# An order for TensorE written by hand through three quarters of a fused attention and FFN kernel, and router gates moved behind the scaling of v

## The chip, the cores and the metric

The kernel runs on one core of a Trainium2 chip. The metric is the device time of one execution in microseconds (us); less is better. TensorE is called PE here, its weight loads PEld, VectorE DVE, ScalarE ACT, GpSimd POOL, and SyncE SP (it issues most DMAs).

## What is computed

Three stages follow each other, for 4 batches of 576 tokens:

```
scores = q @ k^T / 8 + (cum[i] - cum[j])       # 8 heads of 64, causal, cum = cumsum(log f)
x      = softmax(scores) @ v                   # first attention, heads side by side: 512 wide
u      = x + (x^T @ U @ V)^T                   # mixing along the tokens, rank 32
y      = u + relu(u @ w_ch1) @ w_ch2           # FFN, 512 -> 2048 -> 512
logits = y @ w_gate                            # 4 experts, the best 2 chosen per token
out    = sum over chosen e of gate_e * softmax(causal(y wq_e (y wk_e)^T / 8)) @ (y wv_e) @ wo_e
```

## The kernel before

Everything is kept transposed and split into a high and a low part where full precision is wanted, so that most products are made of three matrix products (high x high, high x low, low x high).

**First attention.** The 32 heads go in 16 pairs, numbered 0 to 15 here; four pairs make a batch. For a pair `load_pair`, `split_high` and `split_low` bring q and k into one of two sets of head tiles (`qa, qb, ka, kb`), `value_scale` and `value_parts` scale v and split it (`vh`, `vl`). `row_max` (two PSUM tiles `ua`, `ub`; the maxima on DVE; a turn `mt` on PE; a row `mr` that two DMAs copy into row 66 of `qa`) makes the softmax's maxima ahead of the scores. `scores` makes two PSUM tiles `sc` per head; ACT takes the exponentials (`pf`), ACT makes the high half (`ph`) and DVE the low half (`pl`). `weighted_values` is 45 products into `av`, then DVE normalises into `x`. After both heads `mix` adds the rank-32 product (`gp`, `g`, `up`) and ACT's queue sends the pair's rows of u to DRAM (`udram`).

**FFN.** `ffn_stream` is a generator. Each of its steps is one group of 12 products of 128x288, either `hps` (`ffn_hidden`, line 367) or `cps` (`ffn_out`, line 382); 256 groups make the whole FFN. The weights come in four quarters; `load_quarter_steps` narrows each piece of them on DVE and ACT (tile `wst`) and makes the low half on POOL (`w1l`, `w2l`). `fill(n)` takes n groups; it is called during the first attention from pair 4 on, since batch 0 is through the attention by then. The rest of the FFN runs behind the attention.

**Second attention.** Four experts per batch: `project` (`pq`), `expert_values` (`pv`, then `gates`, `value_scale`, `value_parts`), and the same `row_max`, `scores` and `weighted_values`.

**What sets the order.** In the first attention and the FFN a scheduler orders all engines at build time, by a model of the instructions; the program only says what depends on what. For pair p the program asks for the other head of the pair before and `mix` of it, the maxima of pair p+1 and the scores of pair p in turn, the values of p+1, the inputs of p+2, the first head's weighted values, some steps of the weights (`WRATE`), and then eight FFN groups in one go (none at pair 4, three at pair 15). The second attention is under `tc.manual_schedule` for PE: PE's order there is the program's, with one or two groups of other work (`work_on`) between the steps of a head. On each engine the instructions run in the order they were given, and an instruction that waits holds all that are behind it on its engine.

The PSUM tiles `ua`, `ub`, `sc` share two buffers (`ps2`), `av` has one, and `hps, cps, gp, up, mt, amt, rsp` share three (`psf`).

Of the kernel before, what the change touches and what calls it, by code (L numbers as in the profile page):

```python
# [8 lines left out]
F32 = mybir.dt.float32  # L9
# [8 lines left out]
P = 128  # L18
# [18 lines left out]
VEXP = 8192.0  # L37

WRATE = (0, 0, 1, 4, 4, 4, 3)
FIRST = 0  # L40
LAST = 3
BIG = -1.0e30
NEG = -3.0e38
ISC = 0.125
# [13 lines left out]
def kernel(  # L58
# [417 lines left out]
    def pair_heads(p):  # L476
        return heads[2 * (p % 2)], heads[2 * (p % 2) + 1]
# [43 lines left out]
    def values(p):  # L521
        if p >= NPAIR:
            return
        vr = st_in[p][1]
        st_rs[p] = drain(value_scale(vr[:]))
        value_parts(vr[:], st_rs[p], *vhs[p % 2])

    def maxima(p, j):
        if p < NPAIR:
            cur["last"] = drain(row_max(pair_heads(p)[j], next_mx()))  # L530

    def attend(p, j):
        vh, vl = vhs[p % 2]
# [5 lines left out]
    def mix(p):  # L539

        b, m, x = p // NP, p % NP, xs[p]
        gp = psf.tile([3 * R, P], F32, name="gp", tag="f")
        for t in range(NT):
            k = 64 if t == NT - 1 else P
            nc.tensor.matmul(gp[:], ut[0:k, t, :], x[0:k, t, :], start=t == 0,  # L545
                             stop=t == NT - 1)
        g = sx.tile([3 * R, P], F32R, name="g")
        nc.scalar.copy(g[:], gp[:])
        nc.vector.tensor_tensor(g[R:2 * R, :], gp[R:2 * R, :], f32(g[R:2 * R, :]), OP.subtract)
        ust = sx.tile([P, S], F32, name="ustage")  # L550
        for (t0, t1, c0, c1) in ((0, 2, 0, 256), (2, 5, 256, S)):
            up = psf.tile([P, 512], F32, name="up", tag="f")
            nc.tensor.matmul(up[:, 0:c1 - c0], g[:], vs[:, c0:c1], start=True, stop=False)
            for t in range(t0, t1):
                k = 64 if t == NT - 1 else P
                nc.tensor.matmul(up[:, t * P - c0:t * P - c0 + k], x[0:k, t, :],
                                 ident[0:k, 0:k], is_transpose=True, start=False,
                                 stop=t == t1 - 1)
            nc.scalar.copy(ust[:, c0:c1], up[:, 0:c1 - c0])
        nc.scalar.dma_start(udram[b, :, m, :], ust[:])  # L560
# [1 line left out]
    load_pair(0)  # L562
    split_high(0)
    split_low(0)
    values(0)
    maxima(0, 0)
    maxima(0, 1)
    load_pair(1)
    split_high(1)
    split_low(1)  # L570
# [49 lines left out]
    load_weights(wy_pool, 1)  # L620
    with tc.issue_after(cur["last"].ins):
        load_mix()
    for p in range(NPAIR + 1):
        if p < NPAIR:
            xs[p] = sx.tile([P, NT, P], F32, name="x", bufs=2)
        if p > 0:
            attend(p - 1, 1)
            mix(p - 1)
        if p == NP:
            sin0.release()  # L630
            att0.release()
            pre.release()
            cur["att"] = att
            fu = cur["fu"] = pool("fu", 2, "right")
            fh = cur["fh"] = pool("fh", 8, "right")
            fy = cur["fy"] = pool("fy", 3, "right")
        if p > 0 and p % NP == 0:
            ffn_prepare(p - NP)
            if p == NP:
                ffn_prepare(1)  # L640
        if p == NPAIR:
            break
        maxima(p + 1, 0)
        st_p[p, 0] = drain(scores(pair_heads(p)[0]))
        maxima(p + 1, 1)
        st_p[p, 1] = drain(scores(pair_heads(p)[1]))
        values(p + 1)
        load_pair(p + 2)
        split_high(p + 2)
        split_low(p + 2)  # L650
        attend(p, 0)
        if p < len(WRATE):
            with tc.issue_after(cur["last"].ins):
                more_weights(WRATE[p])
        if p >= NP:
            fill({NP: FIRST, NPAIR - 1: LAST}.get(p, 8))
    hpool.release()
    att.release()
    sin.release()
# [131 lines left out]
    def expert_values(b, y):  # L791

        yh, yl = y
        vr = sy.tile([P, NT, NV], F32, name="vr3", bufs=1)
        v0 = 2 * E * D
        for t in range(NT):
            pv = psf.tile([P, 512], F32, name="pv", tag="f")
            ts_ = slice(t * P, t * P + P)
            n = 0
            for k in range(KT):  # L800
                for ya, wa in ((yh, wah), (yh, wal), (yl, wah)):
                    nc.tensor.matmul(pv[:, 0:NV], ya[:, k, ts_], wa[:, k, v0:v0 + NV],  # L802
                                     start=n == 0, stop=n == 3 * KT - 1)
# [12 lines left out]

    def turn_outputs(b, m, oh, ol):
# [69 lines left out]
    def head_max(h):  # L887
        b, e = divmod(h, E)
        return row_max(pair_of(b, e // 2)[e % 2], next_mx())

    def one(gen):
        next(gen, None)

# [120 lines left out]
```

## Time and profile before

| what | before |
|---|---|
| median of 3 runs | 988.1 us (987.05 to 991.45) |
| the profiled execution, its own time | 991.99 us |
| its span from first to last instruction | 990.1 us |
| PE busy | 885.4 us (89%) |
| DVE / ACT / POOL busy | 558.2 / 414.6 / 286.7 us |
| mean granted PE clock | 0.906 |
| pair 4's first scores | starts at 104.4 us |
| first FFN group | starts at 151.49 us |
| last `mix` ends, the FFN alone follows | 462.5 us |

Busy time counts an instruction from its start to its end. [...] A wait "a <- b" is idle time in front of a that ended when b did.

### The profile page before, as it was taken

To read this page: it belongs to the slowest core of one execution; us is meant where nothing else is said; L and a number is where in the kernel's file an instruction comes from. 1 tells how busy PE (TensorE), PEld (TensorE's weight loads), DVE (VectorE), ACT (ScalarE), POOL (GpSimd) and SP (SyncE) were. 2 spreads that over 40 slices of the span, in tenths; PEclk is the share of its full clock that TensorE was granted. 3 is DMA by queue.
4 is the path that set the end of the run, shared out by engine and by line. 5 is a ranking of instruction groups with operands and counts; after the bars stand their busy time and mean duration, and the time that the engine had idled before them with its cause. 6 is when DMAs were issued, how large, how long until landed. Compare 5 with 4: busy or idle time off the path is not lost.

```text
span 990.1 us, 19003 instructions
## 1 busy us (share of the span) xinstructions
PE 885.4 (89%) x7480; PEld 825.4 (83%) x7480; DVE 558.2 (56%) x1468; ACT 414.6 (42%) x784; POOL 286.7 (29%) x238
## 2 busy tenths in 40 slices
PE   4888878789899998999999999999999686999997
PEld 3777768778888987998998899999998686888875
DVE  7777577877355556453245653222225667666654
ACT  4565555555244444242224342222103543545543
POOL 8444354333332224110324342423022303000010
PEclk9786569889888999899999999999999797989968
DMA  6434445443423242202258663424006220212111
GB/s 182 116 82 123 134 135 165 132 125 105 143 71 85 78 132 66 56 13 74 72 186 300 213 220 112 144 70 126 25 25 180 61 49 7 73 31 74 37 43 55
DMA packets 68777, 101.94 MB, mean 103 GB/s; under 512 B 6608, under 2 KB 49424, under 8 KB 68688
## 3 DMA queue, kind: packets, MB, share of 16 engines
q1 hardware_dynamic: 64416, 92.47, 31.8%
q10 hardware_dynamic: 4272, 8.26, 2.3%
q8 instruction: 59, 0.97, 0.4%
q14 instruction: 30, 0.25, 0.1%
HBM read 60.33 MB, written 22.56 MB: 84 GB/s over the span
## 4 chain that ended last, share of the span: by engine, by line
PE 72%; DVE 13%; DMA 5%; ACT 4%; issue 3%; POOL 2%; SPq 0%; ACTq 0%; POOLq 0%; DVEq 0%
PE hps L367 19%; PE cps L382 19%; PE sc L210 9%; DVE pl L221 3%; PE av L237 3%; PE pq L759 3%; PE pv L802 3%; PE po L838 3%; PE av L241 2%; PE av L239 2%; PE gp L545 2%; DMA ust<-udram 2%; DVE junk L174 2%; PE ub L163 2%; ACT pf L219 1%
## 5 line engine op out<-in xcount | busy, mean ns | idle before, releaser
L382 PE MATMUL cps<-hh,w2h 128*128 128x288 f32 x512 | 153.2, 300 | 4.6 <-DVE yc L384 3.5
L382 PE MATMUL cps<-hh,w2l 128*128 128x288 f32 x512 | 151.6, 296 | 0.0
L382 PE MATMUL cps<-hl,w2h 128*128 128x288 f32 x512 | 150.6, 294 | 0.0
L367 PE MATMUL hps<-uh,w1h 128*128 128x288 f32 x512 | 144.9, 304 | 0.0
L367 PE MATMUL hps<-uh,w1l 128*128 128x288 f32 x512 | 143.5, 301 | 0.0
L221 DVE TENSOR_TENSOR pl<-pf,ph 128x576 f16<-128x576 f32 x144 | 121.4, 850 | 34.7 <-ACT ph L220 34.5
L372 DVE SCALAR_TENSOR_TENSOR hl<-hps,hh 128x288 fp32r<-128x288 f32 x128 | 58.2, 455 | 145.6 <-ACT hh L371 145.5
L371 ACT ACTIVATE hh<-hps 128x288 fp32r<-128x288 f32 x128 | 52.3, 408 | 195.9 <-PE hps L367 190.1
L219 ACT ACTIVATE pf<-sc 128x576 f32<-128x576 f32 x144 | 84.5, 612 | 85.0 <-PE sc L210 64.9
L210 PE MATMUL sc<-qa,ka 67*128 67x288 f32 (+4 forms) x288 | 88.4, 367 | 24.6 <-ACT pf L219 13.1
L237 PE MATMUL av<-vh,ph 128*128 128x65 f16 x720 | 103.6, 211 | 7.1 <-DVE x L283 5.1
L241 PE MATMUL av<-vh,pl 128*128 128x65 f16 x720 | 100.8, 208 | 2.4 <-DVE pl L221 1.7
L239 PE MATMUL av<-vl,ph 128*128 128x64 f16 x720 | 101.5, 207 | 0.0
L382 PEld LDWEIGHTS cps<-hh,w2h 128*128 128x128 f32 x512 | 96.4, 189 | 5.7 <-DVE yc L384 4.1
L367 PEld LDWEIGHTS hps<-uh,w1h 128*128 128x128 f32 x512 | 98.8, 193 | 1.2 <-issue 0.9
L367 PEld LDWEIGHTS hps<-uh,w1l 128*128 128x128 f32 x512 | 99.2, 194 | 0.0
L382 PEld LDWEIGHTS cps<-hh,w2l 128*128 128x128 f32 x512 | 96.3, 188 | 0.0
L382 PEld LDWEIGHTS cps<-hl,w2h 128*128 128x128 f32 x512 | 96.3, 188 | 0.0
L237 PEld LDWEIGHTS <-ph 128*128 128x128 f16 x720 | 74.5, 107 | 19.3 <-DVE x L283 4.7
L220 ACT CAST ph<-pf 128x576 f16<-128x576 f32 x144 | 88.9, 639 | 1.7
L367 PE MATMUL hps<-ul,w1h 128*128 128x288 f32 x512 | 89.2, 297 | 0.0
L210 PEld LDWEIGHTS sc<-qa,ka 67*128 67x128 f32 x288 | 60.3, 231 | 30.0 <-ACT pf L219 15.1
(160 smaller groups left out, 2018.1 us busy)
## 6 DMA issues: line engine op xcount, KB each, us to landing
raw<-in_w_dram SPq DMA_DIRECT2D x32, 512.0 KB
ust<-udram SPq DMA_DIRECT2D x22, 576.0 KB
qkt<-in_qk_dram SPq DMA_DIRECT2D x16, 576.0 KB
yc<-ydram SPq DMA_DIRECT2D x14, 576.0 KB
ydram<-yc SPq DMA_DIRECT2D x14, 576.0 KB
vr<-in_v_dram SPq DMA_DIRECT2D x16, 320.0 KB
udram<-ustage ACTq DMA_DIRECT2D x16, 288.0 KB
ydram<-ust SPq DMA_DIRECT2D x8, 576.0 KB
```

What stands on the lines that cost most here:

```text
L210: nc.tensor.matmul(ps[:, bk, off:off + w], wa, xa, start=bk not in banks[:n], stop=bk not in banks[n + 1:])
L219: nc.scalar.activation(pfv, view, AF.Exp, scale=ISC)
L220: nc.scalar.copy(ph[:, o0:o0 + n], pf[:, 0:n])
L221: nc.vector.tensor_tensor(pl[:, o0:o0 + n], pf[:, 0:n], ph[:, o0:o0 + n], OP.subtract)
L237: nc.tensor.matmul(av[0:m, it, :], ph[0:k, c:c + m], vh[0:k, jt, :], start=first, stop=False)
L239: nc.tensor.matmul(av[0:m, it, 0:64], ph[0:k, c:c + m], vl[0:k, jt, :], start=False, stop=False)
L241: nc.tensor.matmul(av[0:m, it, :], pl[0:k, c:c + m], vh[0:k, jt, :], start=False, stop=last)
L367: nc.tensor.matmul(ph[:], wa[:, k, fs], xa[:, k, :], start=n == 0, stop=n == 3 * KT - 1)
L371: nc.scalar.activation(hh[:], ph[:], AF.Relu)
L372: nc.vector.scalar_tensor_tensor(hl[:], ph[:], 0.0, f32(hh[:]), OP.max, OP.subtract)
L382: nc.tensor.matmul(pc[:], wa[:, t, dsl], xa[:], start=n == 0, stop=n == 3 * FT - 1)
L759: nc.tensor.matmul(pq[:], wa[:, k, w0:w0 + P], ya[:, k, cs], start=n == 0, stop=n == 3 * KT - 1)
```

## The change

Two parts.

1. Pairs 4 to 15 of the first attention are put under `tc.manual_schedule` for PE (`later_batches`). `values`, `maxima`, `mix` and the scores become generators that are taken step by step, and the FFN groups are taken one at a time between these steps: `GROUPS` says how many in each pair (0 in pair 4, then 6, 7, 7, seven times 8, and 3), 79 in all and one more near the end. The other engines are still ordered by the scheduler.
2. In `expert_values` the call of `gates` moves from in front of `value_scale` to behind `value_parts`.

```
-        st_rs[p] = drain(value_scale(vr[:]))
+        st_rs[p] = yield from value_scale(vr[:])
...
-            cur["last"] = drain(row_max(pair_heads(p)[j], next_mx()))
+            cur["last"] = yield from row_max(pair_heads(p)[j], next_mx())
...
         nc.vector.tensor_tensor(g[R:2 * R, :], gp[R:2 * R, :], f32(g[R:2 * R, :]), OP.subtract)
+        yield
...
-FIRST = 0
-LAST = 3
+GROUPS = (0,) * 5 + (6, 7, 7) + (8,) * 7 + (3,)
...
+        for p in range(NP, NPAIR):
+            some = [1] * GROUPS[p]
+
+            def group():
+                if some:
+                    fill(some.pop())
...
+            vals = values(p + 1)
+            mixing = mix(p - 1)
+            sc = pair_scores(p, 0)
+            one(sc)
+            group()
+            one(m1)
+            one(sc)
+            group()
+            m0 = maxima(p + 1, 0)
+            one(m0)
+            group()
+            attend(p - 1, 1)
+            one(vals)
+            group()
+            one(mixing)
+            sc = pair_scores(p, 1)
+            one(sc)
+            one(vals)
+            group()
+            one(m0)
+            one(mixing)
...
+            one(sc)
+            next_inputs(p + 2)
+            group()
+            m1 = maxima(p + 1, 1)
+            one(m1)
+            one(vals)
+            group()
+            attend(p, 0)
+            group()
+            weights_after(p)
+            fill(len(some))
+        attend(NPAIR - 1, 1)
+        fill(1)
+        drain(mix(NPAIR - 1))
+        ffn_prepare(NPAIR - NP)
+
+    with tc.manual_schedule(engines={mybir.EngineType.PE}):
+        later_batches()
...
-        cf = gates(vr[:, :, E * D:NV])
         vh = sy.tile([P, NT, E, 65], F16, name="vh3")
...
-        st_v[b] = (vh, vl, rs, cf)
+        st_v[b] = (vh, vl, rs, gates(vr[:, :, E * D:NV]))
```

Three places show how the instructions move. Line numbers of the changed kernel are one less up to its line 550 or so, and some 60 more in the second attention; a number behind a name tells tiles apart.

**PE, the first FFN groups.** Before: they stand inside the weighted values (`av`) of pair 5's second head, four of them almost in a row.

```order
L239 MATMUL av_2102<-vl1_178,ph_1817 128x64
L260 MATMUL rsp_1858<-ar_1854,ones1_87 128x1
L367 MATMUL hps_1971<-uh_1433,w1h_275 128x288
L367 MATMUL hps_1971<-uh_1433,w1l_276 128x288
...
L367 MATMUL hps_1971<-ul_1434,w1h_275 128x288 x4
L367 MATMUL hps_1988<-uh_1433,w1h_275 128x288
L367 MATMUL hps_1988<-uh_1433,w1l_276 128x288
...
L367 MATMUL hps_1988<-ul_1434,w1h_275 128x288 x4
```

After: the first one stands behind the first scores of pair 5, and the next step of the attention follows it.

```order
L240 MATMUL av_1579<-vh0_174,pl_1349 128x65
L209 MATMUL sc_1669<-qa2_152,ka2_154 128x288
L209 MATMUL sc_1669<-qb2_153,kb2_155 128x288
...
L209 MATMUL sc_1669<-maskt_77,identb_75 128x128
L366 MATMUL hps_1679<-uh_1508,w1h_275 128x288
L366 MATMUL hps_1679<-uh_1508,w1l_276 128x288
...
L366 MATMUL hps_1679<-ul_1509,w1h_275 128x288 x4
L178 MATMUL mt_1696<-ident_72,mx0_92 5x128
L209 MATMUL sc_1702<-qa2_152,ka2_154 128x320
```

The first group moves ahead by most of a pair, and it is now the only other work between two score tiles of one head. The first `cps` group, 12 products in one piece, stands in pair 5 as well, between its last scores and the maxima of pair 6; before, the scheduler had cut it in pieces in pair 6.

**PE, a later pair.** Before, inside the weighted values of pair 8's second head: three groups in a row behind the step that spreads the scale of v (`rsp`).

```order
L260 MATMUL rsp_3098<-ar_3094,ones1_87 128x1
L367 MATMUL hps_3175<-uh_1439,w1h_279 128x288
L367 MATMUL hps_3175<-uh_1439,w1l_280 128x288
...
L367 MATMUL hps_3175<-ul_1440,w1h_279 128x288 x4
L382 MATMUL cps_3192<-hh_2466,w2h_281 128x288
...
L382 MATMUL cps_3192<-hl_2825,w2h_281 128x288
L367 MATMUL hps_3206<-uh_1439,w1h_279 128x288
L367 MATMUL hps_3206<-uh_1439,w1l_280 128x288
...
```

After, in pair 9: one group between steps of the attention. `gp` and `up` are two steps of `mix`, `amt` turns the maxima of v, `mt` those of the scores.

```order
L381 MATMUL cps_3389<-hl_3165,w2h_281 128x288
L548 MATMUL gp_3403<-x_2838,ut_273 96x128 x5
L209 MATMUL sc_3414<-qa3_160,ka3_162 128x288
...
L209 MATMUL sc_3414<-maskt_77,identb_75 128x128
L250 MATMUL amt_3424<-ident_72,am_3387 1x128
L366 MATMUL hps_3430<-uh_3072,w1h_275 128x288
L366 MATMUL hps_3430<-uh_3072,w1l_276 128x288
...
L366 MATMUL hps_3430<-ul_3073,w1h_275 128x288 x4
L178 MATMUL mt_3447<-ident_72,mx1_94 5x128
L557 MATMUL up_3454<-vs_274,g_3409 128x256
L560 MATMUL up_3454<-ident_72,x_2838 128x128 x2
```

Groups that stood several in a row now stand singly; between `gp` and the `up` that needs its result there are one score tile, `amt`, one group and `mt`. From the first group to the last `mix` the order has 83 groups before and 80 now: three move behind it.

**DVE, the gates of batch 0.** Before: `gt`, `eq`, `gmx` are the first of the gates; `am` is the maximum of v, and PE's `amt` waits for it.

```order
L727 TENSOR_TENSOR gt_9349<-vr3_9242 128x80
L728 TENSOR_TENSOR eq_9350<-vr3_9242 128x80
L735 TENSOR_REDUCE gmx_9357<-vr3_9242 128x5
L248 TENSOR_REDUCE am_9372<-vr3_9242 128x1
L729 TENSOR_TENSOR eq_9350<-eq_9350,tie_8025 128x80
L737 TENSOR_TENSOR gex_9359<-vr3_9242,gmx_9357 128x20
L221 TENSOR_TENSOR pl_9338<-pf_9345,ph_9337 128x576
L221 TENSOR_TENSOR pl_9338<-pf_9387,ph_9337 128x512
L731 TENSOR_TENSOR gt_9349<-gt_9349,eq_9350 128x80
L253 TENSOR_REDUCE ar_9397<-amt_9395 1x1
```

After: `am` is first, but the scheduler has set the gates' first three directly behind it, in front of `ar`, for which PE's next step (`rsp`) waits.

```order
L247 TENSOR_REDUCE am_9355<-vr3_9245 128x1
L791 TENSOR_TENSOR gt_9405<-vr3_9245 128x80
L792 TENSOR_TENSOR eq_9406<-vr3_9245 128x80
L799 TENSOR_REDUCE gmx_9413<-vr3_9245 128x5
L220 TENSOR_TENSOR pl_9341<-pf_9348,ph_9340 128x576
L252 TENSOR_REDUCE ar_9380<-amt_9378 1x1
L793 TENSOR_TENSOR eq_9406<-eq_9406,tie_8028 128x80
L801 TENSOR_TENSOR gex_9415<-vr3_9245,gmx_9413 128x20
L165 ISA junk_9392,mx3_98<-ua_9384,maskm_82 128x576
L165 ISA mx3_98 128x1
```

The gates pass from in front of `am` to between `am` and `ar`; the same in the other three batches.

## Rows read from the trace of the kernel before

**Rows 1.** the page: busy time, share of the span and instructions of each engine
```profile
PE 885.4 (89%) x7480; PEld 825.4 (83%) x7480; DVE 558.2 (56%) x1468; ACT 414.6 (42%) x784; POOL 286.7 (29%) x238
```

**Rows 2.** stretches: us; busy (x) of PE, PEld, DVE, ACT, POOL; PEclk, DMA, GB/s
```profile
104.40:462.20 357.80, 321.82 (x2875) 295.02 (x2874) 217.52 (x588) 167.13 (x313) 115.63 (x84) 0.88 0.34 98
104.40:127.90 23.50, 18.22 (x121) 15.62 (x120) 15.04 (x43) 13.98 (x25) 7.58 (x6) 0.57 0.57 169
104.40:218.00 113.60, 93.55 (x776) 83.92 (x775) 79.91 (x203) 63.92 (x116) 48.50 (x32) 0.79 0.47 135
218.00:247.80 29.80, 27.89 (x261) 25.63 (x262) 23.66 (x63) 15.35 (x30) 12.45 (x9) 0.94 0.41 121
247.80:283.90 36.10, 31.48 (x249) 29.04 (x245) 16.24 (x48) 14.82 (x26) 11.33 (x7) 0.76 0.38 115
316.90:354.40 37.50, 37.00 (x373) 34.89 (x371) 19.94 (x58) 13.40 (x27) 9.77 (x7) 1.00 0.33 94
475.00:500.00 25.00, 25.00 (x190) 25.00 (x189) 7.32 (x16) 5.40 (x10) 5.53 (x3) 1.00 0.15 49
836.00:881.00 45.00, 43.60 (x440) 39.34 (x439) 30.34 (x91) 22.01 (x47) 0.19 (x2) 1.00 0.23 60
```

**Rows 3.** one head's weighted values alone: us; PE and DVE busy (x), PEclk
```profile
456.30:458.10 1.80, 1.77 (x45) 0.00 (x0) 1.00 0.00 0
```

**Rows 4.** PE's waits, first attention, 104 to 462 us: total, times, longest us
```profile
PE sc L210 <- ACT pf L219: 7.6, 8, 2.1
PE up L553 <- DVE g L549: 4.8, 4, 2.9
PE gp L545 <- DVE x L283: 4.8, 6, 1.9
PE sc L210 <- DMA qa<-mr: 3.2, 3, 1.7
```

**Rows 5.** timeline, batch 0 on its way to the first FFN group
```profile
117.27 0.34 ACTq L560 DMA_DIRECT2D udram<-ustage  x1
127.15 5.41 POOL L353 TENSOR_TENSOR ul<-ust,uh 128x1152 fp32r<-128x1152 f32 x2 [4.60 <-ACT uh L352]
```

**Rows 6.** timeline of POOL: last low half of the first quarter's weights
```profile
171.27 1.28 POOL L342 TENSOR_TENSOR w2l<-wst,w2h 128x512 fp32r<-128x512 f32 x1
```

**Rows 7.** DVE's groups from 104.4 to 218 us: the weights' three steps, and hl of the groups
```profile
L306 DVE SCALAR_TENSOR_TENSOR wst<-raw,wst 128x512 int32<-128x512 int32 x12 | 9.5, 788 | 1.7 <-ACT raw L305 1.5
L307 DVE SCALAR_TENSOR_TENSOR wst<-raw,wst 128x512 int32<-128x512 int32 x12 | 9.0, 752 | 0.1
L304 DVE TENSOR_SCALAR wst<-raw 128x512 int32<-128x512 int32 x12 | 5.8, 484 | 4.0 <-POOL w1l L342 1.7 <-DMA raw<-in_w_dram 1.5 <-POOL w2l L342 0.6
L372 DVE SCALAR_TENSOR_TENSOR hl<-hps,hh 128x288 fp32r<-128x288 f32 x10 | 4.5, 453 | 5.5 <-ACT hh L371 5.5
```

**Rows 8.** line L221 from 104.4 to 218 us: ns least/median/most
```profile
L221 DVE TENSOR_TENSOR pl<-pf,ph x22: 670/743/2287, 112.3 to 211.4; 128x512 f16<-128x512 f32 x14, 128x576 f16<-128x576 f32 x8
```

**Rows 9.** PE's waits of the second attention, 751 to 990 us
```profile
PE amt L251 <- DVE eq L729: 15.8, 3, 7.9
```

**Rows 10.** timeline: gates and am, batch 0; POOL beside; gates of batch 2
```profile
769.79 5.20 POOL L707 TENSOR_TENSOR yl<-yst,yh 128x1152 fp32r<-128x1152 f32 x2 [0.65 <-ACT yh L706]
771.07 1.45 DVE L727 TENSOR_TENSOR gt<-vr 128x80 f32<-128x80 f32 x1 [2.01 <-ACT vr L805]
772.44 2.65 DVE L728 TENSOR_TENSOR eq<-vr 128x80 f32<-128x80 f32 x1
775.10 1.47 DVE L248 TENSOR_REDUCE am<-vr 128x1 f32<-128x1280 f32 x1
881.92 0.24 DVE L727 TENSOR_TENSOR gt<-vr 128x80 f32<-128x80 f32 x1 [1.57 <-ACT vr L805]
```

**Rows 11.** timeline: an am of the first attention beside a subtraction on POOL
```profile
146.17 0.80 DVE L248 TENSOR_REDUCE am<-vr 128x1 f32<-128x640 f32 x1
146.46 1.40 POOL L518 TENSOR_TENSOR qb<-qkt,qb 64x576 fp32r<-64x576 f32 x1
```

More of the change, by code (lines that the diff above doesn't have):

```diff
@@ L529, in maxima, with one @@
         if p < NPAIR:
-            cur["last"] = drain(row_max(pair_heads(p)[j], next_mx()))
+            cur["last"] = yield from row_max(pair_heads(p)[j], next_mx())
+    def one(gen):
+        next(gen, None)
     def attend(p, j):
@@ L564 @@
     split_low(0)
-    values(0)
-    maxima(0, 0)
-    maxima(0, 1)
+    drain(values(0))
+    drain(maxima(0, 0))
+    drain(maxima(0, 1))
     load_pair(1)
@@ L622, with weights_after @@
         load_mix()
[L623 to L651, printed above, removed]
+    def weights_after(p):
         if p < len(WRATE):
@@ L654, with next_inputs, pair_scores @@
                 more_weights(WRATE[p])
-        if p >= NP:
-            fill({NP: FIRST, NPAIR - 1: LAST}.get(p, 8))
+    def next_inputs(p):
+        load_pair(p)
+        split_high(p)
+        split_low(p)
+    def pair_scores(p, j):
+        st_p[p, j] = yield from scores(pair_heads(p)[j])
+    for p in range(NP):
+        xs[p] = sx.tile([P, NT, P], F32, name="x", bufs=2)
+        if p > 0:
+            attend(p - 1, 1)
+            drain(mix(p - 1))
+        drain(maxima(p + 1, 0))
+        drain(pair_scores(p, 0))
+        drain(maxima(p + 1, 1))
+        drain(pair_scores(p, 1))
+        drain(values(p + 1))
+        next_inputs(p + 2)
+        attend(p, 0)
+        weights_after(p)
@@ new lines, in later_batches @@
+    def later_batches():
+        m0 = m1 = iter(())
+        for p in range(NP, NPAIR):
[3 more added lines that the diff above has]
+                    fill(some.pop())
+            xs[p] = sx.tile([P, NT, P], F32, name="x", bufs=2)
+            if p == NP:
+                cur["att"] = att
+            vals = values(p + 1)
[9 more added lines that the diff above has]
+            group()
+            attend(p - 1, 1)
+            one(vals)
[7 more added lines that the diff above has]
+            one(mixing)
+            if p == NP:
+                sin0.release()
+                att0.release()
+                pre.release()
+                cur["fu"] = pool("fu", 2, "right")
+                cur["fh"] = pool("fh", 8, "right")
+                cur["fy"] = pool("fy", 3, "right")
+            if p % NP == 0:
+                ffn_prepare(p - NP)
+                if p == NP:
+                    ffn_prepare(1)
+            one(sc)
+            next_inputs(p + 2)
+            group()
[3 more added lines that the diff above has]
+            group()
+            attend(p, 0)
+            group()
+            weights_after(p)
+            fill(len(some))
[3 more added lines that the diff above has]
+        ffn_prepare(NPAIR - NP)
@@ L657 @@
+    with tc.manual_schedule(engines={mybir.EngineType.PE}):
+        later_batches()
+    fu, fh, fy = cur["fu"], cur["fh"], cur["fy"]
     hpool.release()
@@ L889, in head_max @@
         return row_max(pair_of(b, e // 2)[e % 2], next_mx())
-    def one(gen):
-        next(gen, None)
     work = []
```

## The prediction

> **What bounds the kernel now.** I read the page's busy times first: PE is busy for 89% of the span and no other engine for more than 56% [rows 1], so time is lost where PE waits or runs slowly. The table of stretches then tells where. From pair 4's first scores to the last mix, 104.4 to 462.2 us, lie 357.8 us; PE was busy for 321.82 of them at a mean granted clock of 0.88 [rows 2]. [...] So 74.6 us of this stretch are loss: 36.0 us in which PE stood still and 38.6 us of half clock. That is what an order of PE can win back here, and no more. The FFN alone, 475 to 500 us, has none to give (25.00 of 25.00 us busy, clock 1.00) [rows 2].
>
> The waits of PE in that stretch are many and small: scores behind the exponential that frees their PSUM tile, `up` behind `g`, `gp` behind the normalised `x`, scores behind the row of maxima [rows 4]. All are round trips PE, ACT or DVE, PE that had no other PE work in front of them, while eight FFN groups stood together elsewhere. The two extremes show what follows: 247.8 to 283.9 us lost 4.6 us of waits and ran at clock 0.76; 316.9 to 354.4 us, with 14 groups in it, lost 0.5 us and ran at 1.00 [rows 2]. That hand-written order with other work between the steps runs well is seen in the second attention, which has one: 836 to 881 us, busy 43.60 of 45.00 us at clock 1.00 [rows 2].
>
> [...]
>
> **The change, part by part.** PE's products are the same, so I cost the stretch from pair 4 on again, pair by pair.
>
> *A pair at full clock.* From 316.9 to 354.4 us PE was busy 37.00 us at clock 1.00 with one pair's scores, maxima and mix, three heads' weighted values and 14 groups (168 products) [rows 2]. A product of a group takes 25.00/190 = 0.1316 us [rows 2], a group 1.58 us; one head's weighted values take 1.77 us [rows 3]. A pair with 8 groups is 37.00 - 6 x 1.58 - 1.77 = 25.7 us; without groups 13.1 us.
>
> *Pair 4* has no groups, as before. The pair without groups took 23.5 us, at clock 0.57 [rows 2]; it now has 2.0 us more of weighted values (37 products at half clock), 25.5 us. Its first scores come directly behind the turn of the maxima, where a head's weighted values stood between: one wait for the row's DMA, the longest of its kind, 1.7 us [rows 4].
>
> *Pairs 5 to 7* have 6, 7 and 7 groups: 22.6 + 24.2 + 24.2 = 71.0 us of PE work. Here DVE also narrows the FFN weights, so I check it: 79.91 us of DVE work now lie between 104.4 and 218.0 us [rows 2]. Four more groups (0.45 us of `hl` or of the sum each [rows 7], 1.8) and three more steps of weights (0.788 + 0.752 + 0.484 = 2.02 us each [rows 7], 6.1) fall into pairs 4 to 7 by the new order, 87.8 us. The best DVE share of a stretch with weights is 23.66/29.8 = 0.79 [rows 2], which makes 111 us, against 1.7 + 25.5 + 71.0 = 98.2 from PE. I take 111: DVE sets these four pairs. With PE alone it is 98 (lower end), with the mean share of the same stretch today (79.91/113.6 = 0.70) 125 (upper end). On SP's queue the weights' loads now follow the row of the next pair's first head instead of the second's, so they leave earlier; a row behind a load that waits for its buffer would be late, a kind of wait that costs 3.2 us today [rows 4], and I book nothing more for it.
>
> *Pairs 8 to 14*: 7 x 25.7 = 179.9 us, plus 3% as in the clean stretch of the second attention (45.00/43.60), 5.4 us. That stretch has no mix, so its two waits are added. They cost 9.6 us over 12 mixes now [rows 4], 0.8 each; with a group in front of `gp` and one in front of `up` I take half, 2.8 us for seven pairs. Bounds: none, or as now, 5.6.
>
> *Pair 15 and the end*: 13.1 us, 3 groups (4.7), one more head and one more mix (4.3), less the maxima of a next pair (1.8), 20.3. The last mix has one group of cover and the last head's scores none: three waits of 1 to 2 us [rows 4], about 5. Together 25.
>
> Sum: 111 + 179.9 + 5.4 + 2.8 + 25 = 324.1 us instead of 357.8: 33.7 us gained. Three groups more follow the stretch, in the FFN where PE is full: 3 x 1.58 = 4.7 us back. Net 29.0 us.
>
> *The gates.* PE waits 15.8 us for `eq` in front of `amt` [rows 9], and it is tempting to book all of it. The order of DVE says otherwise: the scheduler sets `gt` and `eq` directly behind `am`, in front of `ar`, and `rsp` on PE waits for that. What is long there is no arithmetic: in batch 0 `gt` and `eq` take 1.45 and 2.65 us, in batch 2 `gt` takes 0.24, and in batch 0 `eq` ends at 775.09, just when POOL's two subtractions end at 774.99 [rows 10]. `am`, 1.47 us, starts only at 775.10 [rows 10]. A maximum is not held by POOL: another ran in 0.80 us beside a subtraction [rows 11]. So `am` now runs from 771.07 while POOL still holds the two comparisons, and all behind them moves ahead by 1.45 us. This happens in batches 0 and 1; in the two others only the comparisons' own time counts, some 0.3 us of two that overlap (0.24 the first [rows 10]). Sum 2 x 1.45 + 2 x 0.3 = 3.5 us, and the wait goes from `amt` to `rsp`. Bounds: 0 (all of it waits again) and 15.8.
>
> Total 29.0 + 3.5 = 32.5 us. Against the profiled execution's 992.0 us (span 990.1 and 1.9 around it) that is 959.5; the median of the runs is 988.1, 3.9 below it, so I predict **955.6 us**.
>
> **The rivals.**
>
> *More is won* (0.14). DVE does not hold pairs 4 to 7, since it is only the waiting for PE that spreads its work today: 98 instead of 111, and the end loses nothing: 955.6 - 13 - 5 = 938. For it: DVE's share of 0.79 is no ceiling that a row shows. Against: in-order waits behind ACT and POOL in the same rows [rows 7].
>
> *DVE holds longer* (0.16). Pairs 4 to 7 take 125 us (share 0.70), and each later pair 1 us more: 955.6 + 14 + 7 = 977. For it: DVE's subtraction `pl` takes 670 ns at least but up to 2287 [rows 8], and `gt` and `eq` above show who stretches it: POOL, whose 48.50 us now meet DVE's work in fewer us [rows 2]. [...]
>
> *Nothing is won* (0.05). The order doesn't do what it says: one group of 1.58 us is too short a cover, the round trips reappear at every step, and the loss of 74.6 us stays [rows 2]. For it: waits of up to 2.9 us [rows 4] are longer than a group. Against: the second attention's clean stretch has no longer cover between its steps. 988.
>
> *Slower* (0.08). PE's order is fixed, so one late input stops everything. The place is the first group and the first `cps`. Today the inputs of batch 0 are complete some 12 us after the pair's rows leave (117.27, first `ul` 127.15 and 2.7 us) [rows 5], and the first quarter's weights are narrowed at 172.55 us [rows 6]. By my sum PE comes to the first group near 133 us and to the first `cps`, most of a pair later, near 150. If the weights keep today's pace it stands 22 us there; then the gain is only some 10 us. It turns into a loss if the idle PE also keeps the half clock and half of the ten following pairs run like 247.8 to 283.9 us, 36.1 us instead of 27: 955.6 + 5 x 9 = 1000. It decides at a mean of 31 us for pairs 5 to 14. Against: the new order of DVE has the weights' steps ahead of the groups that need them, and nothing before pair 4 is later.
>
> **How the numbers follow.** My case has 0.57, with 943 to 970 us by the bounds of its terms. The range 936 to 980 takes in most of the cases on either side and leaves out slower and no change. Within 0.5% (4.9 us, about what a measurement of this kernel can tell) is the case of nothing, 0.05; slower is 0.08; all others are faster, 0.87.
>
> **What would show it.** Right: the stretch from pair 4 to the last mix near 324 us; its clock above 0.93; the first group near 135 us; pairs 8 to 14 at 26 to 28 us each; pairs 4 to 7 near 111 us with a DVE share near 0.79; `amt` waiting little and `rsp` some 4 us in batches 0 and 1, together 3 to 4 us less; the FFN alone as before. Wrong: long waits at the first `cps` for `w2l`; a clock that still halves in pairs 8 to 14, which would mean that single groups don't cover; a second attention that gains much more than 4 us.

## The result, and the profile after

The changed kernel takes 963.8 us (median), the kernel before 988.0 in the same comparison: a ratio of 0.974, 95% interval 0.970 to 0.979. The forecast was 955.6, its range 936 to 980. The gain is 24.2 us where 32.5 were booked. One of the four runs of the changed kernel took 1068.9 us at a mean granted clock of 0.73; the ratio leaves it out, the median has it in.

The two profiled executions lie further apart than the medians: 960.9 us (span 959.2) against 992.0 (span 990.1), 31 us. Each is at its own end of what its kernel shows, so some 7 us of that difference are a matter of which execution was profiled. The page of the changed kernel, its line of busy times (answers to [rows 1]):

```profile
PE 862.3 (90%) x7480; PEld 804.7 (84%) x7480; DVE 554.7 (58%) x1468; ACT 416.5 (43%) x784; POOL 286.7 (30%) x238
```

The table of stretches of the changed kernel (columns as in [rows 2]): all up to pair 4's first scores, then pair 4 to the last mix, pairs 4 to 7, pair 4, pair 5, pair 8, pair 9, pair 11, pairs 8 to 14, pair 15 with the end, the FFN to the second attention, and the second attention.

```profile
0.00:99.50 99.50, 69.97 (x583) 59.77 (x583) 76.39 (x209) 54.70 (x98) 55.29 (x68) 0.90 0.46 132
99.50:435.80 336.30, 304.21 (x2891) 277.97 (x2891) 217.61 (x593) 168.45 (x311) 116.19 (x84) 0.92 0.36 105
99.50:218.20 118.70, 100.79 (x867) 90.56 (x868) 88.78 (x218) 67.36 (x123) 51.81 (x35) 0.81 0.47 139
99.50:125.70 26.20, 20.25 (x157) 17.50 (x157) 18.00 (x42) 14.23 (x26) 9.56 (x7) 0.57 0.48 149
125.70:163.50 37.80, 30.04 (x233) 26.90 (x231) 26.44 (x59) 18.97 (x35) 17.79 (x11) 0.77 0.46 132
218.20:245.50 27.30, 25.70 (x259) 23.62 (x256) 20.16 (x59) 13.46 (x25) 8.52 (x7) 1.00 0.45 131
245.50:275.50 30.00, 27.31 (x255) 25.19 (x254) 17.48 (x49) 14.86 (x27) 14.74 (x9) 0.94 0.41 112
302.10:328.60 26.50, 25.55 (x255) 23.57 (x255) 16.61 (x49) 12.79 (x24) 7.29 (x6) 1.00 0.27 78
218.20:411.20 193.00, 182.27 (x1778) 168.31 (x1775) 119.36 (x353) 91.91 (x169) 60.07 (x39) 0.98 0.33 95
411.20:435.80 24.60, 21.16 (x255) 19.10 (x253) 9.47 (x23) 9.18 (x19) 4.31 (x12) 1.00 0.04 13
435.80:747.00 311.20, 305.23 (x2283) 303.91 (x2283) 121.20 (x258) 88.28 (x168) 93.17 (x72) 0.99 0.44 138
747.00:959.20 212.20, 182.87 (x1729) 163.02 (x1726) 139.54 (x408) 105.06 (x208) 22.02 (x14) 0.92 0.19 50
```

The same table of the kernel before, for the pieces that [rows 2] doesn't have: up to pair 4, pair 4 to the end of the last mix, pairs 8 to 14, pair 15 with the end, the FFN to the second attention, the second attention.

```profile
0.00:104.40 104.40, 75.17 (x634) 64.57 (x634) 78.05 (x218) 54.44 (x97) 55.81 (x68) 0.79 0.45 126
104.40:462.50 358.10, 322.12 (x2877) 295.21 (x2876) 217.52 (x588) 167.28 (x313) 115.63 (x84) 0.88 0.34 98
218.00:428.40 210.40, 196.21 (x1766) 181.10 (x1766) 122.50 (x350) 90.92 (x173) 61.39 (x39) 0.90 0.32 93
428.40:462.50 34.10, 32.36 (x337) 30.18 (x337) 15.11 (x38) 12.44 (x26) 5.74 (x13) 1.00 0.03 10
462.50:768.50 306.00, 299.18 (x2247) 297.63 (x2247) 121.02 (x255) 87.11 (x166) 93.13 (x72) 1.00 0.44 140
768.50:990.10 221.60, 188.94 (x1729) 168.01 (x1726) 141.61 (x408) 105.77 (x208) 22.13 (x14) 0.88 0.18 48
```

Read side by side, the 30.9 us between the spans are: 4.9 before pair 4, 21.8 from pair 4 to the last mix, 5.2 given back in the FFN, 9.4 in the second attention. The pieces of the stretch also exchanged work. Pairs 4 to 7 took 118.7 us where they had taken 113.6 [rows 2], with 91 products more; pair 15 with the end took 24.6 instead of 34.1, with 82 fewer. The clean gain is in pairs 8 to 14, 193.0 us instead of 210.4 with 12 products more. There PE stood still for 10.7 us instead of 14.2; the other 13.9 us of the gain are busy time, at a clock of 0.98 instead of 0.90. Loss, by the prediction's estimate of it (length less busy time times clock), falls in the stretch from 74.6 to 336.3 - 304.21 x 0.92 = 56 us; there is plenty left. (The product is a rough measure. No run shows that busy time goes with the clock in proportion: in the changed kernel the 128x288 products of a group start 0.24 us apart at a clock of 0.50, from 127.75 to 129.19 us, and 0.133 apart at 1.00, from 450.14 to 451.87 us, so 1.8 times and not twice; and for the same 2891 products it comes to 280 us here and to 270 in experiment 3.) Where PE still waits there (answers to [rows 4]; total, times, longest us):

```profile
PE ub L162 <- ACT pf L218: 8.4, 9, 3.6
PE gp L548 <- DVE x L282: 5.6, 4, 3.2
PE hps L366 <- POOL ul L352: 4.6, 3, 2.3
PE up L557 <- ACT ustage L563: 4.2, 9, 0.5
...
PE cps L381 <- ACT w2h L340: 1.8, 1, 1.8
...
PE cps L381 <- POOL w2l L341: 1.3, 1, 1.3
```

And in the second attention, where [rows 9] had 15.8 us of `amt` behind `eq`:

```profile
PE amt L250 <- DVE am L247: 7.1, 3, 3.9
PE ub L162 <- ACT pf L218: 6.0, 6, 3.5
PE rsp L259 <- DVE ar L254: 4.5, 4, 1.9
```

The wait did not leave with the comparisons. 7.1 us of it stay at `amt`, now behind `am` itself, where little was forecast; `rsp` waits 4.5 us (2.5 before), 2.6 of them in batches 0 and 1, where some 4 were forecast; and `ub` waits 6.0 (2.8 before), which was not forecast.

### The profile page after: what moved, and what is told of

It is laid out like the page before. It is cut to its first block, busy times and chain, and to the rows that moved or that the text cites. A ratio compares the mean times of both kernels' runs of the same rounds, so it can differ in the third digit from the quotient of the medians.

```text
span 959.2 us, 19001 instructions
## 1 busy us (share of the span) xinstructions
PE 862.3 (90%) x7480; PEld 804.7 (84%) x7480; DVE 554.7 (58%) x1468; ACT 416.5 (43%) x784; POOL 286.7 (30%) x238
## 3 DMA queue, kind: packets, MB, share of 16 engines
q1 hardware_dynamic: 64416, 92.47, 32.7%
## 4 chain that ended last, share of the span: by engine, by line
PE 67%; DVE 12%; DMA 8%; ACT 6%; issue 4%; POOL 2%; SPq 1%; ACTq 0%; POOLq 0%; DVEq 0%
PE hps L366 19%; PE cps L381 18%; PE sc L209 8%; PE pq L823 4%; PE pv L866 3%; DMA ust<-udram 2%; DVE pl L220 2%; PE po L901 2%; PE av L236 2%; PE gp L548 2%; PE ub L162 2%; ACT pf L218 2%; DVE junk L173 2%; PE av L240 2%; PE av L238 2%
## 5 line engine op out<-in xcount | busy, mean ns | idle before, releaser
L381 PE MATMUL cps<-hh,w2h 128*128 128x288 f32 x512 | 156.3, 306 | 5.6 <-DVE yc L383 3.7
L220 DVE TENSOR_TENSOR pl<-pf,ph 128x576 f16<-128x576 f32 x144 | 117.7, 823 | 51.8 <-ACT ph L219 51.2
L366 PE MATMUL hps<-uh,w1h 128*128 128x288 f32 x512 | 145.3, 305 | 0.2 <-ACT uh L351 0.2
L236 PE MATMUL av<-vh,ph 128*128 128x65 f16 x720 | 91.9, 206 | 1.9 <-DVE x L282 1.6
L238 PE MATMUL av<-vl,ph 128*128 128x64 f16 x720 | 90.5, 202 | 0.0
L240 PE MATMUL av<-vh,pl 128*128 128x65 f16 x720 | 90.0, 202 | 0.1
L209 PE MATMUL sc<-qa,ka 67*128 67x288 f32 (+4 forms) x288 | 83.0, 348 | 7.9 <-ACT pf L218 3.8
L236 PEld LDWEIGHTS <-ph 128*128 128x128 f16 x720 | 70.9, 104 | 13.7 <-issue 5.6
L173 DVE CUSTOM_DVE_ANT_0 junk<-ub,maskm 128x448 bf16<-128x448 f32 x192 | 79.6, 414 | 3.2 <-PE ub L162 1.2
```

The lines of the kernel that those rows point to most:

```text
L173: nc.vector.tensor_tensor_reduce(junk[0:n, 0:w], ub[0:n, bk, off:off + w], maskm[0:n, m0:m0 + w], 1.0, NEG, OP.add, OP.max, mx[0:n, t:t + 1])
L209: nc.tensor.matmul(ps[:, bk, off:off + w], wa, xa, start=bk not in banks[:n], stop=bk not in banks[n + 1:])
L220: nc.vector.tensor_tensor(pl[:, o0:o0 + n], pf[:, 0:n], ph[:, o0:o0 + n], OP.subtract)
L236: nc.tensor.matmul(av[0:m, it, :], ph[0:k, c:c + m], vh[0:k, jt, :], start=first, stop=False)
L238: nc.tensor.matmul(av[0:m, it, 0:64], ph[0:k, c:c + m], vl[0:k, jt, :], start=False, stop=False)
L240: nc.tensor.matmul(av[0:m, it, :], pl[0:k, c:c + m], vh[0:k, jt, :], start=False, stop=last)
```

## The experiments

The granted clock is a share of the full one; the clock records of the traces before and after hold two values of it, 1.0 and 0.5. "Us of half clock" in the expectations are stretches at 0.5, 32.6 us of the changed kernel's second attention (212.2 us at a mean of 0.92). Each run's ratio is against the kernel before on the same chip.

**1 and 2. The gates by themselves, and the change without them.** In the kernel before, and in reverse in the changed one:

```
         vh = sy.tile([P, NT, E, 65], F16, name="vh3")
-        cf = gates(vr[:, :, E * D:NV])
...
-        st_v[b] = (vh, vl, rs, cf)
+        st_v[b] = (vh, vl, rs, gates(vr[:, :, E * D:NV]))
```

> The kernel before with the gates alone moved behind the halves of v; the first attention keeps the planner's order. Theory (the forecast's term): 3.5 us less than before, near 984.5; in the second attention the waits on the comparisons go, those on the scale's row (rsp) and on the exponential (ub) rise. Rival (the second attention of the changed kernel is 9.4 us shorter in the profiles, and the gates did all of it): 9 us less, near 979. Rival (moved waits only): within 1 us of before.

> The changed kernel with the gates put back in front of the halves of v. Theory: 3.5 us more than the changed kernel's 963.8, near 967.5, and the first attention as in the changed kernel. Rival (gates did all of the second attention's 9.4 us): near 973. Rival (the order of the first attention shifted the second's clock): within 1 us of 963.8.

Gates alone: 978.9 us, ratio 0.994 (0.991 to 0.998), 7.0 us under the median before of 985.9. The change without them: 971.0, ratio 0.985 (0.979 to 0.991), where the whole change has 0.974; a hundredth of 988 more, 10.6 us. The second attention is 211.4 us with the gates behind and 222.0 with them in front, whatever the first attention's order is; first the row of the gates alone, then that of the change without them:

```profile
763.10:974.50 211.40, 181.42 (x1729) 161.61 (x1726) 137.32 (x408) 105.10 (x208) 22.08 (x14) 0.92 0.19 50
```
```profile
750.40:972.40 222.00, 189.74 (x1729) 168.78 (x1726) 141.38 (x408) 105.71 (x208) 22.03 (x14) 0.88 0.18 48
```

The first interval, 2 to 9 us, holds both the forecast's 3.5 and the rival's 9; those of the second comparison touch at 0.979. It is the profiles that speak for the rival: 10.6 us between these two rows. Waits make up the smaller part: length less busy time is 32.7 us in front (before) and 29.3 behind (changed kernel), 3.3 us. The other 6 us are busy time that shrank from 188.9 to 182.9 for the same 1729 products: the clock of 0.92 instead of 0.88.

**3. The order kept, the groups not between the steps.**

```
             def group():
-                if some:
-                    fill(some.pop())
+                pass
```

> The changed kernel, its hand-written order of PE kept, but each pair's FFN groups stand together at the end of the pair, where the planner had put most of them. Theory (single groups as cover are the gain): the waits behind the exponential, x, g and the maxima come back, the stretch from pair 4 to the last mix goes from 336 us to 360 or more, the granted clock in it to 0.88 or below, the whole near 988. Rival (the order of the steps alone is enough): within 5 us of 963.8.

1040.2 us, ratio 1.055 (1.048 to 1.062): not back to the kernel before, as expected, but 54 us worse than it. The stretch from pair 4 to the last mix:

```profile
101.40:513.20 411.80, 355.05 (x2891) 323.58 (x2891) 229.19 (x593) 167.47 (x310) 116.91 (x84) 0.76 0.29 86
```

and its longest waits of PE:

```profile
PE gp L548 <- DVE x L282: 32.6, 12, 6.4
PE ub L162 <- DVE mx L165: 21.9, 22, 1.2
```

The same 2891 products as in the changed kernel take 75.5 us longer. `gp` waits for `x` once in every pair, 2.7 us, and `ub` for the maxima twice, 1.0 us each, and the clock is 0.76. A fixed order has nothing to set against a wait but the work in front of it. What wins is what stands between the steps, and a group of 1.58 us does it.

**4. Every group one slot later.** GROUPS from `(6, 7, 7) + (8,) * 7 + (3,)` to `(5, 7, 7) + (8,) * 7 + (4,)`. The reason is pair 9 above: 30.0 us where pair 11 has 26.5. The timeline of PE in the changed kernel, and POOL's beside it, show what is late:

```profile
247.14 0.29 PE L366 MATMUL hps<-uh,w1l 128*128 128x288 f32 x1
249.29 0.79 PE L366 MATMUL hps<-ul,w1h 128*128 128x288 f32 x4 [1.86 <-POOL ul L352]
```
```profile
245.11 1.42 POOL L518 TENSOR_TENSOR kb<-qkt,kb 64x576 fp32r<-64x576 f32 x1 [5.55 <-DMA kb<-kb]
246.61 2.63 POOL L352 TENSOR_TENSOR ul<-ust,uh 128x1152 fp32r<-128x1152 f32 x1
```

The first group of a new batch comes directly behind the pair's first scores, and its `ul` is still being made; POOL had `kb` in front of it. Pair 13 repeats it with 2.3 us.

> The changed kernel with one group fewer in pair 5 and one more in pair 15, so that every group from there on stands one slot later, and the first one of a new batch no longer directly behind the first scores of pairs 9 and 13. Theory (pairs 9 and 13 are 3.5 us longer than their neighbours since PE waits 1.9 and 2.3 us for ul there and then runs 3.4 us at half clock): both go, 7.6 us less in all, near 956. Rival (the half clock there has another cause): only the waits go, near 960. Rival (ul is still late one slot on, or pair 5 loses its cover): within 1.5 us of 963.8.

958.4 us, ratio 0.974 (0.967 to 0.981), no different from the changed kernel's. Pair 13 fell from 30.4 to 27.5 us at clock 1.00, so the reading of `ul` holds there. Pair 9 fell only to 28.7: `ul` was in time, and `cps` waited 2.0 us for `hl` instead. What was won at pairs 5 and 7 came back in pair 8, which took 36.3 us: PE waited 3.1 us for `w2h` of the second quarter and 3.3 us for an exponential that stood on ScalarE behind a split of the next inputs, late itself. Pairs 4 to 8 together took 146.0 us, the same as in the changed kernel (99.5 to 245.5).

**5 to 7. What sets pairs 4 to 8?** Three runs: weights two steps earlier (WRATE from `(0, 0, 1, 4, 4, 4, 3)` to `(0, 1, 2, 4, 4, 4, 1)`); one VectorE instruction per step of weights instead of three, which leaves the low bits and the sign out,

```
-            narrow(st[:], raw[:].rearrange("p (n two) -> p n two", two=2), DM)
+            nc.vector.tensor_scalar(st[:].bitcast(I32), hi, 2, None, OP.logical_shift_right)
+            nc.scalar.activation(f32(lo), f32(hi), AF.Copy, scale=2.0 ** -112)
```

and a warm PE in pair 4, in each of its eight slots:

```
+                    junk = psf.tile([P, HC], F32, name="junkp", tag="f")
+                    for n in range(24):
+                        nc.tensor.matmul(junk[:, 0:P], identb[:], maskt[:], start=n == 0,
+                                         stop=n == 23)
```

> The changed kernel with two of the FFN weights' steps moved from pair 6 to pairs 1 and 2 (WRATE), so that the first quarter's second half is narrowed about half a pair earlier. Theory (pair 5 takes 37.8 us instead of 26.7 because the weights are late: 3.1 us on w2h and w2l directly, 3.6 us on an exponential that stands in ScalarE's queue behind w2h, and half clock after them): pair 5 near 29 us, pairs 1 to 3 at most 3 us longer together, near 957. Rival (VectorE is the bound, the work is only moved): pairs 1 to 3 grow by what pair 5 loses, within 2 us of 963.8.

> The changed kernel with one VectorE instruction of three per step of FFN weights (the two that put in the low bits and the sign are left out, so the weights are other numbers): 1.24 us less VectorE work per step, about 11 us less in pairs 4 to 7. Forecast's step (VectorE sets pairs 4 to 7): they fall from 118.7 us by 11/0.75 = 15 to about 104, the whole near 949. Rival (the weights' waits in pair 5 alone): pair 5 falls by some 8 us, the others stay, near 956. Rival (neither: half clock and round trips set these pairs): pairs 4 to 7 stay within 3 us of 118.7.

> The changed kernel with 24 superfluous products of 128x128 without a reader in each of the eight group slots of pair 4, which has no groups (about 1.3 us a slot at full clock, twice that at half; nothing else changes). Theory (pairs 4 and 5 lose most by half clock, 22.8 and 17.4 us of it, because pair 4 leaves PE idle): pair 4 stays within 3 us of 26.2, pair 5 falls to about 31, the whole near 959. Rival (the clock follows something else, or the weights set pair 5): pair 4 grows by 10 us or more and pair 5 stays, near 974.

Weights earlier: 968.6 us, ratio 0.977 (0.972 to 0.983), no gain. Pair 5 fell from 37.8 to 31.1, near the 29 expected, but pairs 4, 6 and 8 grew by 3.2, 3.5 and 3.4; pairs 4 to 8 took 147.8. Light weights: 957.0, ratio 0.968 (0.964 to 0.973). Pairs 4 to 8 of that run:

```profile
101.20:245.10 143.90, 125.75 (x1120) 113.42 (x1121) 87.68 (x246) 81.97 (x150) 59.36 (x40) 0.84 0.49 139
```

VectorE's busy time there fell from 108.9 us (changed kernel) to 87.7, and the length from 146.0 to 143.9. Work taken from an engine that sets a stretch comes off its length; here a tenth of it did (the changed kernel's own two profiles differ by 0.7 us). Pair 5 lost its waits for the weights (31.3 us), pair 6 took 33.4, with 3.4 us on `x`.

The warm pair 4: 971.4 us, ratio 0.982 (0.977 to 0.988), slower than the changed kernel. Its pairs 4 and 5:

```profile
98.40:124.60 26.20, 25.01 (x348) 23.51 (x349) 15.83 (x41) 14.40 (x26) 9.62 (x7) 0.91 0.47 146
124.60:165.70 41.10, 28.21 (x232) 23.95 (x230) 26.86 (x61) 20.00 (x36) 19.59 (x13) 0.82 0.49 137
```

The theory holds for pair 4, which ran at 0.91 instead of 0.57 and stayed at 26.2 us, and falls for pair 5, which took 41.1 us where 31 were expected. PE came to the first `cps` at 149.0 us instead of 153.7 and stood there for `w2h` and `w2l`, 8.5 us in all. What the raised clock alone is worth in pair 4 this run cannot tell: the 192 superfluous products kept PE busy for 13.10 us of it, 1.64 a slot, where the expectation's 1.3 at full clock was an estimate, and with them PE was busy for 25.01 of the 26.20 us, so they may have used up what the clock gave.

**8. Gates further back still,** held behind the scaling of v:

```
-        value_parts(vv_, rs, vh, vl)
-        st_v[b] = (vh, vl, rs, gates(vr[:, :, E * D:NV]))
+        scaled = value_parts(vv_, rs, vh, vl)
+        with tc.issue_after(scaled.ins): st_v[b] = (vh, vl, rs, gates(vr[:, :, E * D:NV]))
```

> The changed kernel with the gates held back behind the scaling of v, so that nothing of them stands on VectorE between the maximum am and the scale's last step ar, nor in front of the first subtraction pl. Theory (in batch 0 the first comparison, 2.62 us beside GpSimd, holds pl, with it the exponential's buffer and the maxima, on which TensorE waits 3.5 us, and two short ones hold ar): the waits on the exponential (6.0 us in the second attention) and on ar (4.5) fall to about half, 5 us less, near 959; with half clock spared besides, up to 8 us less. Rival (the gates now hold the halves of q instead): within 1.5 us of 963.8.

968.3 us, ratio 0.979 (0.975 to 0.983). `rsp` waits 0.3 us instead of 4.5, but `ub` still 5.7, and new waits came (`pq` for `qb` 2.3, `op` for `kb` 1.2): in sum nothing. The second attention took 219.5 us, at the clock of the gates in front:

```profile
748.80:968.30 219.50, 190.05 (x1728) 168.75 (x1726) 142.52 (x408) 105.85 (x208) 22.48 (x14) 0.89 0.18 48
```

**9 to 11. Both small moves at once, with one and with two groups, and the changed kernel again.**

> Both small moves at once: one group from pair 5 to pair 15, and two steps of the weights from pair 6 to pairs 1 and 2. Theory (pairs 4 to 8 end, 146 us after pair 4's start, when the chain of the weights through VectorE, ScalarE and GpSimd ends, and each move alone only shifted the place of the wait): with the weights earlier and the groups later, the first product of the second quarter finds its w2h, pairs 4 to 8 fall to about 138, pairs 9 and 13 to 27 to 28.7; 8 to 10 us less than the changed kernel on the same chip. Rival (rows that stand behind the weights' loads on SP's queue set these pairs): pairs 4 to 8 stay at 144 or more, 2 us less.

> As the run before it, with two groups from pair 5 to pair 15 instead of one. Theory: as there, ul now late nowhere (pairs 9 and 13 at 26.6 both); within 2 us of it. Rival (rows behind the loads): pairs 4 to 8 stay at 144 or more. Rival (pair 5 needs its groups as cover): pair 5 as long as with one group more, and the whole 2 to 3 us slower than the run before.

> The changed kernel again, unchanged, beside the two others on one chip. It shows how far the second attention's length moves from one profiled execution to another with the same instructions: 212.2 us with 32.6 us of half clock in the profile of the changed kernel, 218.0 us with 53.3 in the run with superfluous products, whose second attention has the same instructions. Theory (what the gates win for sure is 3 us of waits; the other 6 us are a clock that falls differently from execution to execution): between 211 and 219 us. Rival (the clock belongs to the order): within 1.5 us of 212. The whole: 0.974 of the kernel before.

One group: 957.4 us, ratio 0.969 (0.965 to 0.974). Two: 965.8, 0.979 (0.973 to 0.985), with pairs 4 to 8 at 149.3 us. The changed kernel again: 962.3, 0.973 (0.968 to 0.977). The first is 4.9 us faster than the changed kernel beside it by the medians, but the intervals overlap, and not by its theory: pairs 4 to 8 took 147.8 us, not 138. Now `gp` waited there for `x`, 14.6 us in four waits. Nothing shows that it beats the changed kernel.

The second attention of the changed kernel, run again, took 211.2 us at 0.92, like the 212.2 above. In all but one of the eleven profiles with the gates where the change puts them it took 211 to 213 us; in the warm run, whose second attention is written the same, 218.0 at 0.88.

**12. The weights' loads off SP's queue.** SP's queue issues the loads of weights, inputs and rows in one order. In pairs 4 to 8 of the changed kernel (99.5 to 245.5) its longest wait is a load of weights whose buffer VectorE has not yet freed:

```profile
SPq L324 <- DVE wst L306: 25.3, 6, 6.4
SPq L182 <- DVE hl L371: 15.7, 4, 8.7
```

In this run they are issued on ScalarE's queue (`nc.scalar.dma_start` in `read`).

> The changed kernel with the loads of the FFN weights (raw) issued from ScalarE's queue, where each stands directly behind the copy w1h or w2h, instead of SP's. Theory (in pairs 4 to 7 the weights' loads wait on SP's queue for VectorE to free their buffer, 33 us in the changed kernel, and the rows of the inputs and maxima stand behind them; that, not VectorE's share, holds pairs 4 to 8 at 144 to 148 us in four variants): pairs 4 to 8 fall to 136 or less, TensorE's waits for x and for the exponential in them to half, the whole 8 to 12 us less, near 953. Rival (the chain of the weights through the three engines sets these pairs, the queue is only where it shows): pairs 4 to 8 stay at 142 or more, the whole within 4 us of 963. Rival (ScalarE's own queue now holds the exponentials): slower than 966.

959.7 us, ratio 0.975 (0.970 to 0.980). The waits of those loads are gone from SP's queue, but the queue's wait for the maxima's row (`mr`) rose there from 0.2 to 22.4 us; pairs 4 to 8 take 143.0 us; PE's waits for `x` in them are longer, not shorter:

```profile
PE gp L548 <- DVE x L282: 12.3, 4, 6.0
```

By its own bounds the first theory (136 or less) falls: the 143.0 us are 3.0 less than the changed kernel's 146.0.

## Why the prediction was right, and where it was not

**Where the time is** was right for pairs 8 to 14: the loss lay in round trips and half clock, and single groups between the steps take most of it away. Experiment 3 shows that it is the groups, not the order of the steps: 336.3 us with them, 411.8 without. The rival that nothing is won, because one group is too short, falls with it: pairs 8 to 14 are 17.4 us shorter, at a clock of 0.98. For the whole stretch the clock was to be above 0.93; it is 0.92, and pairs 4 to 7, at 0.81, hold it down. Pair 9, the prediction's bad extreme with 36.1 us, takes 30.0; five of the seven pairs 8 to 14 lie between 25.6 and 27.3, where 26 to 28 were booked.

| step of the forecast | forecast | measured |
|---|---|---|
| pair 4 | 25.5 + 1.7 | 26.2 |
| pairs 5 to 7 | 83.8 | 92.5 |
| pairs 8 to 14 | 188.1 | 193.0 |
| pair 15 and the end | 25 | 24.6 |
| groups moved to the FFN | 4.7 | 5.2 |
| gates, gain | 3.5 | 9.4 |

**The step that failed** is "DVE sets these four pairs". Its work was counted well (87.8 forecast, 88.78 measured), its share was not 0.79 but 0.75, and its mechanism was wrong: with a fifth less VectorE work pairs 4 to 8 are 2 us shorter. The 7.7 us that pairs 4 to 7 are over the forecast lie in pair 5: `ub` waits 3.6 us for an exponential which stands behind `w2h` in ScalarE's queue, `cps` 3.1 us for `w2h` and `w2l`, and the clock is 0.77. That is the place which the rival "slower" named, with 3.1 us where it had 22: the first quarter's last `w2l` was done at 158.6 us instead of 172.6. With it falls the rival that VectorE holds longer: 118.7 lies between its 125 and my 111, but not by its mechanism. The rival that more is won had its premise right, that VectorE does not hold these pairs, and its time, 98, was further off than mine. The 37 products moved into pair 4 come to 2.9 us by [rows 3] if half clock doubles their time, not to the 2.0 booked; there they took 2.2, at a clock of 0.57. The first group came at 127.4 us, earlier than the 133 to 135 forecast, and it came into the half clock (0.50 from 127.0 to 130.5 us).

What does set pairs 4 to 8 stays open. The changed kernel took 146.0 us for them and 145.3 when run again; groups one slot later (experiment 4), earlier weights (5), less VectorE work (6), both moves (9) and another queue (12) gave 146.0, 147.8, 143.9, 147.8 and 143.0; the kernel before took 143.4, with 84 products fewer. Each cure removed the wait it was made for, and a wait of like size stood elsewhere, most often `gp` behind `x`. A step of weights passes VectorE, ScalarE, VectorE, ScalarE and GpSimd in turn, in three queues that also carry the pairs' own chains; that fits, but is argued, not shown.

**Pairs 8 to 14** are 4.9 us over. The forecast had no term for the first group of a new batch: `ul` in pairs 9 and 13, 1.9 and 2.3 us, and a clock of 0.94 in both pairs after it. For pair 13 experiment 4 shows it, for pair 9 another wait took its place, and its 28.7 us there are no less than the 28.4 that the changed kernel took when run again, with 1.5 us on `ul`.

**The gates** were mis-sized, and most of what they won came by a way that the forecast had not. The timeline of VectorE, with POOL's subtractions beside it, in batch 0 of the changed kernel (answers to [rows 10]):

```profile
749.57 1.49 DVE L247 TENSOR_REDUCE am<-vr 128x1 f32<-128x1280 f32 x1 [2.01 <-ACT vr L869]
750.97 2.62 DVE L791 TENSOR_TENSOR gt<-vr 128x80 f32<-128x80 f32 x1
753.52 0.23 DVE L792 TENSOR_TENSOR eq<-vr 128x80 f32<-128x80 f32 x1
753.67 0.17 DVE L799 TENSOR_REDUCE gmx<-vr 128x5 f32<-128x20 f32 x1
753.75 0.74 DVE L220 TENSOR_TENSOR pl<-pf,ph 128x576 f16<-128x576 f32 x1
754.42 0.27 DVE L252 TENSOR_REDUCE ar<-amt 1x1 f32<-1x128 f32 x1
```
```profile
748.29 5.21 POOL L771 TENSOR_TENSOR yl<-yst,yh 128x1152 fp32r<-128x1152 f32 x2 [0.65 <-ACT yh L770]
```

As booked, `am` runs beside POOL (1.49 us; 1.47 after POOL's end before [rows 10]), one comparison takes 2.62 us and ends with POOL (753.59 and 753.50), and `ar` stands behind it. Not booked: `pl` stands behind it too, with it an exponential's buffer, and PE waits 3.5 us at `ub`. Taking the comparison away does not free `pl`. In experiment 8 it stands directly behind `am`, takes 2.95 us itself beside POOL's subtractions, and PE still waits 3.1 us at `ub`:

```profile
752.94 2.95 DVE L220 TENSOR_TENSOR pl<-pf,ph 128x576 f16<-128x576 f32 x1
```
```profile
750.06 5.21 POOL L771 TENSOR_TENSOR yl<-yst,yh 128x1152 fp32r<-128x1152 f32 x2 [0.65 <-ACT yh L770]
```

The waits fell by 3.3 us, and that this is nearly the forecast's 3.5 is luck. The table of stretches for batches 0 and 1, then for batches 2 and 3, of the kernel before and of the changed one:

```profile
768.50:881.30 112.80, 92.67 (x866) 85.56 (x864) 75.84 (x213) 54.77 (x107) 16.77 (x11) 0.89 0.19 48
881.30:990.10 108.80, 96.28 (x865) 82.45 (x863) 65.77 (x195) 51.00 (x101) 5.35 (x3) 0.87 0.16 48
```
```profile
747.00:858.60 111.60, 95.65 (x866) 88.63 (x864) 73.50 (x213) 54.25 (x107) 16.80 (x11) 0.88 0.20 49
858.60:959.20 100.60, 87.22 (x865) 74.39 (x863) 66.04 (x195) 50.81 (x101) 5.22 (x3) 0.97 0.18 51
```

In batches 0 and 1 PE stood still for 4.2 us less, where 2.9 were booked, but its busy time grew by 3.0, and they are 1.2 us shorter. In batches 2 and 3, where 0.6 was booked, it stood still for 0.9 us more, and yet they are 8.2 us shorter: busy time at a clock of 0.97 instead of 0.87. So the step that failed here is the term of 3.5 us, which counted waits alone; two thirds of the 9.4 us are a clock that rose where no wait had been taken away, and why it rose stays open. I said that a second attention which gains much more than 4 us would make the prediction wrong; it gained 9.4.

**The sums.** The misses partly cancel: 12.2 us too much in the stretch and 0.5 in the FFN, against 5.9 at the gates and 4.9 ahead of pair 4. That leaves 1.9 over, of which 0.5 is the reading of the stretches' ends. The 4.9 were not booked: 51 products moved out of the first 100 us, 37 of which I had added to pair 4 and not taken off here, and the clock of the first 100 us, 0.90 where it had been 0.79 (pair 4 begins between 98.4 and 103.2 us in seven profiles with the same steps ahead of it). Against the profiled executions the forecast was 959.5, and 960.9 came, 1.4 over. The rest of the 8.2 us are the 2.9 by which the changed kernel's median lies above its profile, and the 3.9 that I took off because the kernel before had its median below.

## What to carry to other kernels

The order written by hand paid only by the work that it set into the round trips; the same order with its filler elsewhere was slower than the planner. Before naming an engine as the bound of a stretch from its busy share, ask what would happen with less work on it: here VectorE had a share of 0.75, and a fifth less work on it took 2.1 us off 146.0. Read a gain stage by stage before naming its cause: the sum of the waits fell as forecast, in other batches than forecast, and most of the time came from the clock of two batches in which the waits had not fallen. And count the new first user of every buffer that a reordering meets, as with the first group of a batch.

## What the runs showed of the hardware

- With nearly the same waits the second attention ran at 0.92 or at 0.88, which is 6 to 10 us. The place is batches 2 and 3, above all batch 3, where the pair that began at 935.6 us before had 0.66 and its counterpart has 0.92:

```profile
935.60:960.60 25.00, 22.40 (x169) 18.69 (x168) 18.01 (x57) 11.13 (x21) 2.52 (x1) 0.66 0.03 12
```
```profile
910.20:931.30 21.10, 17.45 (x171) 14.28 (x169) 18.11 (x57) 11.17 (x21) 2.55 (x1) 0.92 0.04 14
```

PE's waits in the two are 2.6 and 3.6 us, so their sum does not decide it; what does, no run here shows.
- 192 superfluous products, 13.10 us of PE's busy time, went into pair 4 without lengthening it: 26.2 us at 0.57 without them and at 0.91 with them.
- Three VectorE instructions took about as long as each other beside POOL's subtractions: `eq` 2.65 us before [rows 10], `gt` 2.62 in the changed kernel and `pl` 2.95 with the gates further back. With no subtraction beside it `gt` took 0.24 us before, in batch 2 [rows 10], and `pl` 0.74 in the changed kernel after POOL's end.
